# Attention scores of two batches: three float16 products on 64 rows per head in place of stacked operands on 128 rows

## The chip, the cores and the metric

One Trainium2 chip, one of its cores. The time is the device time of that core in microseconds, as a median of runs without a profile; spans, rows and waits come from one further, profiled execution. The core has TensorE for matrix products (PE in the rows, PEld for its weight loads), VectorE (DVE), ScalarE (ACT), GpSimd (POOL) and SyncE (SP), which here issues every DMA.

## The reference, cut to what matters

Rotary attention over 4 batches of 8 heads, 576 positions and 64 numbers per head, and a gated two-layer network on its output:

```python
q_rot, k_rot = (rotate(q), rotate(k))
scores = scale * np.matmul(q_rot, k_rot.transpose(0, 1, 3, 2))
scores = scores - np.max(scores, axis=-1, keepdims=True)
attn = np.exp(scores)
attn = attn / (np.sum(attn, axis=-1, keepdims=True) + 1e-09)
out = np.matmul(attn, v)
...
x = np.ascontiguousarray(out.transpose(0, 2, 1, 3)).reshape(B * S, H * D)
gate = 1.0 / (1.0 + np.exp(-(x @ w_gate)))
val = x @ w_val
return (gate * val @ w_out).astype(np.float32)
```

## The kernel before, in words

Everything is computed on one core. Heads are taken in pairs (`NP` = 4 pairs per batch), one head on partitions 0 to 63 and the other on 64 to 127. For a pair, `keys_queries` loads keys and queries, turns them by the rotary angles and, in batches 2 and 3, splits each into a float16 high part and a float16 rest (`scaled` on ScalarE, `rest` on VectorE). `score_mm` computes the scores of a tile of 128 positions of both heads against all 576 positions, in two column halves of 288; four such tiles and one of 64 positions (t = 4, both heads in one PSUM tile) make a pair. `softmax` reads the scores from PSUM (VectorE, line 505: minimum and copy), takes the exponential (ScalarE, 510), and splits the result into float16 parts; DMA transposes turn it (537), and `weigh` multiplies by the values (matmuls of line 547, target `pv`). `hidden` (matmuls of line 598, target `m`) and `project` (line 632) are the network.

Scores of batches 0 and 1 are float32 products: per column half one matmul for each head, on the 64 rows where the head lies, each of them two MATMUL instructions in a trace (line 470). Scores of batches 2 and 3 are products of float16 parts, high by high, high by rest and rest by high. So that one matmul on all 128 rows does two of these three, eight DMAs per pair (lines 449 to 455) copy the parts from the buffer `sw`, where the split left them, to `stk`, which holds for each head a stack of two parts of the queries and two stacks of the keys; each head then needs two matmuls per column half (line 482), one task for each head. The float32 operands of batches 0 and 1 lie in the same memory as `stk`.

The order of the work is not written by hand. Each piece is a task with an engine, a supposed cost in microseconds and a rank; `Plan` plays these tasks through once, when the kernel is built, and each engine then gets its instructions in the order in which they started there. A changed cost or a merged task can thus move instructions on every engine. On the chip each engine works through its own list in order and waits where data aren't there.

The scores go to two PSUM tiles, `s_ps[0]` and `s_ps[1]`, one for each head of the pair; there is no second pair of them. Three PSUM tiles `m` serve the network.

Of the kernel before, what the change touches and what calls it, by code (L numbers as in the profile page):

```python
# [156 lines left out]
def rope_attention_then_sigmoid_glu(ctx: ExitStack, tc: tile.TileContext, qk, v, w_in, w_out, tables, out):  # L157
# [17 lines left out]
    row = sb("row", [128, 32])  # L175
    pt = [sb(f"pt{i}", [128, 18, (256, 320)[i]], F16) for i in range(2)]

    stk = sb("stk", [128, 3, 2, 3, S], F16)

    flat = stk.rearrange("p n h m c -> p (n h m c)").bitcast(F32)  # L180
    qk0 = [flat[:, 2 * S * n:2 * S * n + 2 * S].rearrange("p (m c) -> p m c", m=2) for n in range(NP)]
    qkr = [sb(f"qk{n}", [128, 2, S]) for n in range(2)]
    sw = [sb(f"sw{n}", [128, 2, S]) for n in range(2)]
    p32 = [sb(f"p32{n}", [128, S]) for n in range(3)]
# [214 lines left out]
    def keys_queries(b, p, rank):  # L399

        z = ring("sw", 2)
        Z = [("sw", z, m) for m in range(2)]
        if b < NW:
            x, X = qk0[p], [("stk", n) for n in range(8 * p, 8 * p + 8)]
            X = [X[0:4], X[4:8]]
        else:
            r = ring("qk", 2)
            x, X = qkr[r], [[("qk", r, m)] for m in range(2)]
        y = sw[z]
        early = -8.5 if b == p == 0 else rank - 0.1  # L410
        dma(early, [], X[0] + X[1], 576, lambda: Y.dma_start(out=x, in_=qk[b, p, 0]))
        dma(early, [], Z, 576, lambda: Y.dma_start(out=y, in_=qk[b, p, 1]))
        gate = ["tab"] + ([("ws", 8 + p)] if b == 1 else [])
        places = [("POOL", c_pool(S, two=True))] if b > 1 else [("DVE", c_dve(S, two=True))]
        for m in range(2):
            either(places, rank, gate, X[m], lambda E, m=m: E.tensor_tensor(  # L416
                out=x[:, m], in0=x[:, m], in1=tab[:, 0], op=ALU.mult))
            either(places, rank, gate, [Z[m]], lambda E, m=m: E.tensor_tensor(  # L418
                out=y[:, m], in0=y[:, m], in1=tab[:, 1], op=ALU.mult))
            either(places, rank, [Z[m]], X[m], lambda E, m=m: E.tensor_tensor(  # L420
                out=x[:, m], in0=x[:, m], in1=y[:, m], op=ALU.add))
        if b < NW:
            slots[b, p] = p, None, -1.0 / D ** 0.5
            return
        X = X[0] + X[1]
        t, k = ring("stk", 3), ring("q_m", 4)
        M = ("q_m", k)
        e16 = y.rearrange("p m c -> p (m c)").bitcast(F16).rearrange("p (n c) -> p n c", n=4)
# [11 lines left out]
        for m, hi, lo in ((0, 1, 2), (1, 0, 3)):  # L440
            op("ACT", c_act(S), rank, [X[m], Q], Z, lambda E, m=m, hi=hi: scaled(A, e16[:, hi], x[:, m], q_s[:, k, m:m + 1]))
            op2(c_dve(S, two=True), rank, [X[m], Q], Z, lambda E, m=m, hi=hi, lo=lo: rest(
                e16[:, lo], x[:, m], q_s[:, k, m:m + 1], e16[:, hi]))
        W = [("stk", n) for n in range(12 * t, 12 * t + 12)]
        for h in range(2):
            U = W[6 * h:6 * h + 6]
            hs = slice(64 * h, 64 * h + 64)
            dst = stk[:, t, h]
            dma(rank, Z, U[0:2], 216, lambda hs=hs, dst=dst: Y.dma_start(
                out=dst[0:64], in_=e16[hs, 0:3]), U)  # L450
            dma(rank, Z, U[2:3], 72, lambda hs=hs, dst=dst: Y.dma_start(
                out=dst[64:128, 0], in_=e16[hs, 3]), U)
            dma(rank, Z, U[3:4], 72, lambda hs=hs, dst=dst: Y.dma_start(
                out=dst[64:128, 1], in_=e16[hs, 2]), U)
            dma(rank, Z, U[4:6], 72, lambda hs=hs, dst=dst: Y.dma_start(
                out=dst[64:128, 2], in_=e16[hs, 1]), U)
        slots[b, p] = t, se, se


    def score_mm(b, p, t, heads, rank):  # L460

        n = slots[b, p][0]
        if b < NW:
            kT, qT = qk0[n][:, 0], qk0[n][:, 1]

            def both(rows, width, to):
                for c in range(2):
                    for e in range(2):
                        hs = slice(64 * e, 64 * e + 64)
                        T.matmul(s_ps[to[e]][hs if width == 64 else slice(0, 128), c, 0:288], lhsT=qT[hs, rows:rows + width],  # L470
                                 rhs=kT[hs, c * 288:c * 288 + 288], start=True, stop=True)
            R = [("stk", m) for m in range(8 * n, 8 * n + 8)]
            to = heads if t < 4 else heads * 2
            mm(0.84 * len(heads), rank, R, [("s", h) for h in heads],
               lambda: both(t * 128, 128 if t < 4 else 64, to))
            return

        def one(e, o, rows, width):
            q, k, ks = (stk[:, n, e, m] for m in range(3))
            for c in range(2):  # L480
                for m, kk in enumerate((k, ks)):
                    T.matmul(o[:, c, 0:288], lhsT=q[:, rows:rows + width], rhs=kk[:, c * 288:c * 288 + 288],  # L482
                             start=(m == 0), stop=(m == 1))
        R = [[("stk", m) for m in range(12 * n + 6 * e, 12 * n + 6 * e + 6)] for e in range(2)]
        if t < 4:
            for e in range(2):
                mm(4 * c_pe(288), rank, R[e], [("s", heads[e])], lambda e=e: one(e, s_ps[heads[e]], t * 128, 128))
        else:
            h = heads[0]
            mm(8 * c_pe(288), rank, R[0] + R[1], [("s", h)], lambda: [  # L490
                one(e, s_ps[h][64 * e:64 * e + 64], 512, 64) for e in range(2)])

    def softmax(b, p, t, u, rank):

# [270 lines left out]
```

## Time and profile before

| | |
|---|---|
| median of three runs | 735.48 us (735.28 to 738.73) |
| span of the profiled execution, first to last instruction | 733.1 us |
| what lies around the span, if that execution ran as the median | 2.4 us |
| TensorE matmul busy | 632.3 us, 86% of the span |
| VectorE busy | 526.3 us, 72% |
| ScalarE busy | 462.8 us, 63% |
| GpSimd busy | 74.8 us, 10% |
| DMA moved | 100.55 MB, 54.4% of 16 engines' span in the main queue |

Busy shares are averages over stages that differ: the first quarter of the span, in which the weights are decoded and batch 0 goes through attention, leaves TensorE idle for long stretches; in most of the rest TensorE has no gap. A row's mean duration of a matmul contains the way through the array, so matmuls that follow each other overlap; the time that one costs in a stream is read from start to start.

### The profile page before, as it was taken

How to read it: one execution, taken by the hardware profiler on the slowest of the kernel's cores; microseconds unless marked ns; L12 is line 12 of the kernel's file. 1: busy time of each engine (PE TensorE's matmuls, PEld its weight loads, DVE VectorE, ACT ScalarE, POOL GpSimd, SP SyncE). 2: the span in 40 equal slices, each digit the busy share in tenths (PEclk: the TensorE clock that was granted, in tenths of full speed). 3: DMA queues.
4: the chain of work that ended last, by engine and by line, in shares of the span. 5: the costliest groups of instructions: out<-in, count | busy, mean ns of one | idle time of the engine just before them, and what ended most of it. 6: DMA issues, size and time to landing. Idle time of an engine off the chain costs nothing.

```text
span 733.1 us, 12435 instructions
## 1 busy us (share of the span) xinstructions
PE 632.3 (86%) x4642; PEld 414.7 (57%) x4642; DVE 526.3 (72%) x1194; ACT 462.8 (63%) x940; POOL 74.8 (10%) x54
## 2 busy tenths in 40 slices
PE   2355885873279999999999999999999999999997
PEld 1133573551146754577657765578667756866753
DVE  6998899988988973688879998688948574421320
ACT  3767899886556984577758768676757564322320
POOL 0400000000031100014313130131300000000000
PEclk9976697786589999999999999999999999999999
DMA  9965744746934174389596779966483534000001
GB/s 365 318 140 148 233 130 165 198 128 175 255 106 130 34 176 113 86 175 190 130 199 140 160 147 195 202 149 138 105 187 90 118 70 115 1 2 29 1 9 35
DMA packets 187484, 100.55 MB, mean 137 GB/s; under 512 B 171040, under 2 KB 176288, under 8 KB 185376
## 3 DMA queue, kind: packets, MB, share of 16 engines
q1 hardware_dynamic: 187424, 99.77, 54.4%
q8 instruction: 36, 0.59, 0.3%
q14 instruction: 24, 0.20, 0.1%
HBM read 43.12 MB, written 4.72 MB: 65 GB/s over the span
## 4 chain that ended last, share of the span: by engine, by line
PE 73%; DVE 18%; DMA 4%; issue 2%; ACT 2%; SPq 0%; DVEq 0%; ACTq 0%
PE m L598 34%; PE m L632 19%; PE pv L547 9%; PE s L470 5%; PE s L482 5%; DVE p L281 3%; DMA pt<-p 3%; DVE p L505 2%; DVE wo L298 2%; DVE wo L302 2%; DVE sw L418 1%; DVE stk L420 1%; DVE w L281 1%; DMA sw<-in_qk_dram 1%; DVE wo L295 1%
## 5 line engine op out<-in xcount | busy, mean ns | idle before, releaser
L598 PE MATMUL m<-xt,w 128*128 128x320 f16 (+1 forms) x2304 | 303.6, 290 | 8.0 <-ACT w L275 2.6
L598 PEld LDWEIGHTS <-w 128*128 128x128 f16 x2304 | 224.9, 99 | 79.2 <-issue 14.9
L632 PE MATMUL m<-wo,gt 128*128 128x512 f16 x648 | 145.9, 380 | 0.0
L510 ACT ACTIVATE p<-p,st 128x576 f32<-128x576 f32 x144 | 110.6, 769 | 51.8 <-DVE p L505 43.4
L281 DVE SCALAR_TENSOR_TENSOR p<-p,st,p 128x576 f16<-128x576 f32 x144 | 117.2, 845 | 21.9 <-ACT p L275 21.3
L470 PE MATMUL s<-stk 64*128 64x288 f32 (+1 forms) x320 | 70.0, 508 | 52.7 <-DVE p L505 38.2
L275 ACT ACTIVATE p<-p,st 128x576 f16<-128x576 f32 x144 | 104.3, 764 | 14.6 <-DVE st L515 3.5
L632 PEld LDWEIGHTS <-gt 128*128 128x128 f16 x648 | 62.1, 98 | 73.1 <-issue 4.0
L547 PE MATMUL pv<-pt,v 128*64 128x256 f16 (+3 forms) x960 | 77.1, 312 | 21.5 <-DMA pt<-p 21.5
L608 DVE SCALAR_TENSOR_TENSOR th<-th,m 128x256 f32<-128x256 f32 (+1 forms) x96 | 43.1, 450 | 67.7 <-PE m L598 66.1
L275 ACT ACTIVATE gt<-th,c_s 128x256 f16<-128x256 f32 (+1 forms) x96 | 50.3, 528 | 50.0 <-DVE th L608 49.5
L547 PEld LDWEIGHTS <-v 128*64 128x64 f16 (+1 forms) x960 | 54.1, 118 | 44.7 <-issue 29.1
L470 PEld LDWEIGHTS s<-stk 64*128 64x128 f32 (+1 forms) x320 | 35.4, 210 | 76.6 <-DVE p L505 47.5
L604 ACT ACTIVATE th<-m,gsc 128x256 f32<-128x256 f32 (+1 forms) x96 | 47.1, 493 | 36.6 <-PE m L598 35.4
L281 DVE SCALAR_TENSOR_TENSOR gt<-th,c_s,gt 128x256 f16<-128x256 f32 (+1 forms) x96 | 53.4, 562 | 19.1 <-ACT gt L275 19.0
L505 DVE TENSOR_SCALAR_CACHE_REDUCE p<-s,q_e 128x576 f32<-128x576 f32 x72 | 57.5, 812 | 10.6 <-PE s L482 10.0
L505 DVE TENSOR_SCALAR_CACHE_REDUCE p<-s 128x576 f32<-128x576 f32 x72 | 53.4, 751 | 15.0 <-PE s L470 14.5
L418 POOL TENSOR_TENSOR sw<-sw,tab 128x576 f32<-128x576 f32 x16 | 25.4, 1590 | 264.7 <-DVE xm L556 174.1
L482 PE MATMUL s<-stk 128*128 128x288 f16 (+1 forms) x320 | 44.4, 288 | 0.4 <-DVE p L505 0.4
L416 POOL TENSOR_TENSOR qk<-qk,tab 128x576 f32<-128x576 f32 x16 | 25.1, 1593 | 181.0 <-DMA qk<-in_qk_dram 137.5
L275 ACT ACTIVATE o<-m,o_s 128x512 f32<-128x512 f32 x16 | 11.0, 685 | 42.2 <-PE m L632 42.0
L482 PEld LDWEIGHTS <-stk 128*128 128x128 f16 (+1 forms) x320 | 27.4, 100 | 13.9 <-issue 5.4
(94 smaller groups left out, 508.8 us busy)
## 6 DMA issues: line engine op xcount, KB each, us to landing
wo<-in_w_dram SPq DMA_DIRECT2D x12, 1024.0 KB, 5.6
sw<-in_qk_dram SPq DMA_DIRECT2D x16, 576.0 KB, 5.1
xt<-in_wo_dram SPq DMA_DIRECT2D x12, 512.0 KB, 4.4
stk<-in_qk_dram SPq DMA_DIRECT2D x8, 576.0 KB, 4.5
xt<-in_v_dram SPq DMA_DIRECT2D x4, 1152.0 KB, 6.6
qk<-in_qk_dram SPq DMA_DIRECT2D x8, 576.0 KB, 6.0
out_dram<-o SPq DMA_DIRECT2D x16, 256.0 KB, 2.2
stk<-sw SPq DMA_DIRECT2D x16, 216.0 KB, 3.6
```

The lines of the kernel that those rows point to most:

```text
L275: A.activation(o, src, AF.Copy, scale=scale)
L281: V.scalar_tensor_tensor(out=o, in0=src, scalar=scale, in1=hi, op0=ALU.mult, op1=ALU.subtract)
L418: either(places, rank, gate, [Z[m]], lambda E, m=m: E.tensor_tensor(out=y[:, m], in0=y[:, m], in1=tab[:, 1], op=ALU.mult))
L470: T.matmul(s_ps[to[e]][hs if width == 64 else slice(0, 128), c, 0:288], lhsT=qT[hs, rows:rows + width], rhs=kT[hs, c * 288:c * 288 + 288], ...
L482: T.matmul(o[:, c, 0:288], lhsT=q[:, rows:rows + width], rhs=kk[:, c * 288:c * 288 + 288], start=(m == 0), stop=(m == 1))
L505: lambda E, h=h, c=c: V.tensor_scalar(out=p32[prs[c]].rearrange("p (c n) -> p c n", c=2), in0=s_ps[h][:, :, 0:288], scalar1=down, scalar2= ...
L510: lambda E, c=c: A.activation(p32[prs[c]], p32[prs[c]], AF.Exp, bias=st[:, k, 0, c:c + 1], scale=-1.0, accum_out=st[:, k, 1, c:c + 1]))
L547: T.matmul(v_ps[64 * e:64 * e + 64, 0:n], lhsT=v16[hs, p, a, g, :], rhs=pt[z][hs, c * 9 + g, 0:n], start=(first and m == 0), stop=(last an ...
L598: T.matmul(m_ps[m][:, 0:n], lhsT=w16[:, f, g, a, cc, :], rhs=x[:, cc, c, c0:c0 + n], start=(k == 0), stop=(k == 11))
L604: op("ACT", c_act(n), rank - 0.05, [("m", m), ("gsc", b, f)], [("th", r)], lambda E, m=m: A.activation(t, m_ps[m][:, 0:n], AF.Tanh, scale= ...
L608: op("DVE", c_dve(n, psum=True), rank - 0.05, [("m", m)], [("th", r)], lambda E, m=m: V.scalar_tensor_tensor(out=t, in0=t, scalar=1.0, in1 ...
L632: T.matmul(m_ps[m], lhsT=gt[:, f, a, c0:c0 + 128], rhs=wo16[:, f, c, :], start=(f == 0 and k == 0), stop=(f == NF - 1 and k == 2))
```

## The change

`stk` and the stacking DMAs go. `big`, four buffers of keys and queries, holds the float32 operands of batches 0 and 1 and, for batches 2 and 3, seen as float16 (`half`), high part and rest of each; the split writes there directly. A score tile of batches 2 and 3 is now one task for both heads: for each of the three terms and each column half one matmul per head, on that head's 64 rows. The supposed costs of the score tasks in `Plan` change too, for batches 0 and 1 as well (1.68 or 0.84 before, 1.2 now), and the buffers that order one task behind another are now the four `big` instead of the three `stk`.

```diff
-    stk = sb("stk", [128, 3, 2, 3, S], F16)
...
+    big = [sb(f"big{n}", [128, 2, S]) for n in range(NP)]
+    half = [t.rearrange("p m c -> p (m c)").bitcast(F16).rearrange("p (m a c) -> p m a c", m=2, a=2) for t in big]
...
-        t, k = ring("stk", 3), ring("q_m", 4)
+        t, k = ring("big", NP), ring("q_m", 4)
...
-        W = [("stk", n) for n in range(12 * t, 12 * t + 12)]
-        for h in range(2):
-            U = W[6 * h:6 * h + 6]
-            hs = slice(64 * h, 64 * h + 64)
-            dst = stk[:, t, h]
-            dma(rank, Z, U[0:2], 216, lambda hs=hs, dst=dst: Y.dma_start(
-                out=dst[0:64], in_=e16[hs, 0:3]), U)
...
+        for m in range(2):
+            h, R = half[t][:, m], [("big", t, m)]
+            op("ACT", c_act(S), rank, [X[m], Q], R, lambda E, m=m, h=h: scaled(A, h[:, 0], x[:, m], q_s[:, k, m:m + 1]))
+            op2(c_dve(S, two=True), rank, [X[m], Q], R, lambda E, m=m, h=h: rest(
+                h[:, 1], x[:, m], q_s[:, k, m:m + 1], h[:, 0]))
...
-            q, k, ks = (stk[:, n, e, m] for m in range(3))
-            for c in range(2):
-                for m, kk in enumerate((k, ks)):
-                    T.matmul(o[:, c, 0:288], lhsT=q[:, rows:rows + width], rhs=kk[:, c * 288:c * 288 + 288],
-                             start=(m == 0), stop=(m == 1))
...
+            todo = [(half[n][:, 0, a], half[n][:, 1, c]) for c, a in TERMS]
+
+        def both():
+            for m, (kT, qT) in enumerate(todo):
                 for c in range(2):
                     for e in range(2):
                         hs = slice(64 * e, 64 * e + 64)
                         T.matmul(s_ps[to[e]][hs if width == 64 else slice(0, 128), c, 0:288], lhsT=qT[hs, rows:rows + width],
-                                 rhs=kT[hs, c * 288:c * 288 + 288], start=True, stop=True)
...
+                                 rhs=kT[hs, c * 288:c * 288 + 288], start=(m == 0), stop=(m == len(todo) - 1),
+                                 skip_group_check=True)
+        mm((0.6 if b < NW else 0.42) * 2, rank, [("big", n, m) for m in range(2)], [("s", h) for h in heads], both)
```

What stands in TensorE's list for the first score tile of batch 2, before the change: the four products of one head (`s_112` is the first head's PSUM tile), with a weight load ahead of each.

```order
3095 L482 LDWEIGHTS stk
3096 L482 MATMUL s_112<-stk 128x288
3097 L482 LDWEIGHTS stk
3098 L482 MATMUL s_112<-stk 128x288
3099 L482 LDWEIGHTS stk
3100 L482 MATMUL s_112<-stk 128x288
3101 L482 LDWEIGHTS stk
3102 L482 MATMUL s_112<-stk 128x288
```

The four of the other head (`s_113`) follow at 3122, behind a small matmul and nine of line 632.

The same tile after the change (line 459 is now the matmul of all scores, `s_115` and `s_116` are the two heads' PSUM tiles, `big_73` is the first `big`):

```order
3078 L459 LDWEIGHTS big_73
3079 L459 MATMUL s_115<-big_73 128x288
3080 L459 LDWEIGHTS big_73
3081 L459 MATMUL s_116<-big_73 128x288
3082 L459 LDWEIGHTS big_73
3083 L459 MATMUL s_115<-big_73 128x288
3084 L459 LDWEIGHTS big_73
3085 L459 MATMUL s_116<-big_73 128x288
```

Sixteen more rows of the same pattern follow, up to 3101: twelve matmuls of both heads in turn, with nothing between them.

On SP's list, in batch 1's attention, the stacking stood between the transposes (537) and the loads of the next pair (411, 412), before the change:

```order
96 L534 DMA p_81<-p_81 64x2x576
97 L412 DMA sw_76<-in_qk_dram 128x1152
98 L449 DMA stk<-sw_77 64x1728 x2
99 L411 DMA qk_75<-in_qk_dram 128x1152
100 L537 DMA_TRANSPOSE pt_72<-p_81 128x18x64
101 L451 DMA stk<-sw_77 64x576 x2
102 L537 DMA_TRANSPOSE pt_72<-p_82 128x18x128
103 L453 DMA stk<-sw_77 64x576 x2
104 L537 DMA_TRANSPOSE pt_72<-p_81 128x18x128
105 L455 DMA stk<-sw_77 64x576 x2
```

After it (the transpose is line 508, the loads are 408 and 409, the copy of the 64-position tile is 505), the list of the same stretch has the loads and the transposes alone:

```order
89 L408 DMA qk_78<-in_qk_dram 128x1152
90 L505 DMA p_84<-p_84 64x2x576
91 L508 DMA_TRANSPOSE pt_72<-p_84 128x18x64
92 L508 DMA_TRANSPOSE pt_72<-p_85 128x18x128
93 L409 DMA sw_80<-in_qk_dram 128x1152
94 L508 DMA_TRANSPOSE pt_72<-p_84 128x18x128
```

VectorE's list also moves. Just ahead of the reduction that ends batch 0's attention (556, last of its eight), before the change:

```order
318 L302 SCALAR_TENSOR_TENSOR wo_62<-wo_62,xt_65 128x512
319 L420 TENSOR_TENSOR stk<-stk,sw_76 128x576
320 L505 TENSOR_SCALAR p_78,st<-s_112 128x576
321 L505 TENSOR_SCALAR p_79,st<-s_113 128x576
322 L416 TENSOR_TENSOR stk<-stk,tab 128x576
323 L281 SCALAR_TENSOR_TENSOR xt_64<-pv,xt_64 128x320
324 L556 TENSOR_REDUCE xm<-xt_64 128x1
```

After it (476 reads the scores, 293 to 300 decode an output weight, 279 is the split, 527 the reduction):

```order
318 L417 TENSOR_TENSOR big_75<-big_75,sw_79 128x576
319 L476 TENSOR_SCALAR p_81,st<-s_115 128x576
320 L476 TENSOR_SCALAR p_82,st<-s_116 128x576
321 L293 TENSOR_SCALAR wo_62<-xt_65 128x512
322 L296 SCALAR_TENSOR_TENSOR wo_62<-wo_62,xt_65 128x512
323 L300 SCALAR_TENSOR_TENSOR wo_62<-wo_62,xt_65 128x512
324 L484 TENSOR_SCALAR st<-st 128x2
325 L279 SCALAR_TENSOR_TENSOR xt_64<-pv,xt_64 128x320
326 L527 TENSOR_REDUCE xm<-xt_64 128x1
```

Over all that stands ahead of that reduction, three decoding instructions and one small one have come in and one multiplication by the rotary table (416) has gone behind it.

## Rows read from the trace of the kernel before

**Rows 1.** Busy time by stretch: engine, us busy, instructions; PEclk is the granted clock.

```profile
core 0 of [0], span 733.1 us
core 0: us, PE busy (x) PEld busy (x) DVE busy (x) ACT busy (x) POOL busy (x), PEclk, DMA share, GB/s
0.00:209.00 209.00, 118.24 (x736) 77.34 (x736) 183.86 (x376) 151.23 (x304) 7.90 (x10) 0.79 0.70 207
209.00:255.00 46.00, 42.72 (x302) 28.69 (x299) 41.40 (x88) 34.52 (x72) 12.92 (x8) 1.00 0.26 65
255.00:606.00 351.00, 348.95 (x2755) 228.62 (x2754) 269.38 (x657) 243.50 (x504) 53.99 (x36) 1.00 0.66 145
606.00:733.00 127.00, 122.42 (x857) 80.09 (x855) 31.67 (x75) 33.52 (x62) 0.00 (x0) 1.00 0.10 27
```

**Rows 2.** TensorE's matmuls by form from 255 to 606 us: busy, mean ns.

```profile
L482 PE MATMUL s<-stk 128*128 128x288 f16 x256 | 39.0, 287 | 0.4 <-DVE p L505 0.4
L470 PE MATMUL s<-stk 64*128 64x288 f32 x96 | 14.9, 429 | 0.0
L482 PE MATMUL s<-stk 128*64 128x288 f16 x64 | 5.5, 292 | 0.0
L470 PE MATMUL s<-stk 64*64 64x288 f32 x32 | 4.8, 415 | 0.0
```

**Rows 3.** Waits of TensorE's matmuls from 255 to 606 us: total, times, longest.

```profile
PE m L598 <- DVE xt L281: 0.7, 1, 0.7
PE m L598 <- ACT th L604: 0.6, 1, 0.6
PE s L482 <- DVE p L505: 0.4, 1, 0.4
PE m L598 <- ACT xt L275: 0.2, 1, 0.2
```

**Rows 4.** The stacking DMAs on SP's queue: durations ns min/median/max, first and last start.

```profile
L449 SPq DMA_DIRECT2D stk<-sw x16: 461/553/1058, 315.7 to 566.6; - x16
...
L455 SPq DMA_DIRECT2D stk<-sw x16: 583/592/602, 326.7 to 580.2; - x16
```

**Rows 5.** VectorE's groups from 255 to 606 us, and three from 100 to 209.

```profile
L505 DVE TENSOR_SCALAR_CACHE_REDUCE p<-s,q_e 128x576 f32<-128x576 f32 x71 | 56.7, 812 | 10.6 <-PE s L482 10.0
L281 DVE SCALAR_TENSOR_TENSOR sw<-qk,q_s,sw 128x576 f16<-128x576 f32 x16 | 12.9, 809 | 0.6 <-ACT sw L275 0.6
...
L298 DVE SCALAR_TENSOR_TENSOR wo<-wo,xt 128x512 int32<-128x512 int32 x10 | 6.9, 692 | 0.7
...
L416 DVE TENSOR_TENSOR stk<-stk,tab 128x576 f32<-128x576 f32 x7 | 5.3, 752 | 0.0
L295 DVE TENSOR_SCALAR wo<-xt 128x512 int32<-128x512 int32 x10 | 4.2, 418 | 0.0
```

**Rows 6.** TensorE's timeline, three stretches: start, us to the last one's end, count.

```profile
395.07 1.14 PE L482 MATMUL s<-stk 128*128 128x288 f16 x8
396.05 1.79 PE L598 MATMUL m<-xt,w 128*128 128x320 f16 x12
397.68 0.66 PE L482 MATMUL s<-stk 128*128 128x288 f16 x4
...
400.51 1.79 PE L598 MATMUL m<-xt,w 128*128 128x320 f16 x12 [0.55 <-ACT th L604]
402.23 2.35 PE L547 MATMUL pv<-pt,v 128*64 128x320 f16 x30
...
416.76 0.69 PE L482 MATMUL s<-stk 128*64 128x288 f16 x8
417.39 0.45 PE L598 MATMUL m<-xt,w 128*128 128x320 f16 x2
```

**Rows 7.** The same for single pairs of a float32 score tile, in narrow windows.

```profile
343.03 0.51 PE L470 MATMUL s<-stk 64*128 64x288 f32 x2
...
343.37 0.41 PE L470 MATMUL s<-stk 64*128 64x288 f32 x2
...
343.62 0.41 PE L470 MATMUL s<-stk 64*128 64x288 f32 x2
```

**Rows 8.** Weight loads by form from 255 to 606 us: busy, mean ns.

```profile
L482 PEld LDWEIGHTS <-stk 128*128 128x128 f16 x256 | 24.2, 98 | 11.5 <-issue 3.0
L470 PEld LDWEIGHTS s<-stk 64*128 64x128 f32 x96 | 8.3, 186 | 4.2 <-issue 1.9 <-DVE st L513 0.5 <-DVE gt L281 0.4
```

**Rows 9.** The first pair of a 64-position tile, and the first two, in narrow windows.

```profile
416.76 0.33 PE L482 MATMUL s<-stk 128*64 128x288 f16 x2
...
416.76 0.45 PE L482 MATMUL s<-stk 128*64 128x288 f16 x4
```

**Rows 10.** The chain that ended last, near the end of batch 0's attention.

```profile
195.06 4.89 DMA p<-p
...
199.97 3.92 DMA pt<-p
...
203.93 4.26 PE pv L547 x28
```

**Rows 11.** SP's transposes from 185 to 206 us: durations ns min/median/max.

```profile
L537 SPq DMA_TRANSPOSE pt<-p x3: 1723/2020/5512, 185.6 to 200.0; - x3
```

More of the change, by code (lines that the diff above doesn't have):

```diff
@@ L176, in rope_attention_then_sigmoid_glu @@
     pt = [sb(f"pt{i}", [128, 18, (256, 320)[i]], F16) for i in range(2)]
-    stk = sb("stk", [128, 3, 2, 3, S], F16)
-    flat = stk.rearrange("p n h m c -> p (n h m c)").bitcast(F32)
-    qk0 = [flat[:, 2 * S * n:2 * S * n + 2 * S].rearrange("p (m c) -> p m c", m=2) for n in range(NP)]
+    big = [sb(f"big{n}", [128, 2, S]) for n in range(NP)]
+    half = [t.rearrange("p m c -> p (m c)").bitcast(F16).rearrange("p (m a c) -> p m a c", m=2, a=2) for t in big]
     qkr = [sb(f"qk{n}", [128, 2, S]) for n in range(2)]
@@ L403, in keys_queries @@
         if b < NW:
-            x, X = qk0[p], [("stk", n) for n in range(8 * p, 8 * p + 8)]
-            X = [X[0:4], X[4:8]]
+            x, X = big[p], [[("big", p, m)] for m in range(2)]
         else:
@@ L425, in keys_queries @@
         X = X[0] + X[1]
-        t, k = ring("stk", 3), ring("q_m", 4)
+        t, k = ring("big", NP), ring("q_m", 4)
         M = ("q_m", k)
-        e16 = y.rearrange("p m c -> p (m c)").bitcast(F16).rearrange("p (n c) -> p n c", n=4)
         for m in range(2):
@@ L439, in keys_queries @@
             out=se, in0=q_i[:, k, 0:1], scalar=-1.0 / D ** 0.5, in1=q_i[:, k, 1:2], op0=ALU.mult, op1=ALU.mult))
[L440 to L443, printed above, removed]
-        W = [("stk", n) for n in range(12 * t, 12 * t + 12)]
-        for h in range(2):
-            U = W[6 * h:6 * h + 6]
-            hs = slice(64 * h, 64 * h + 64)
-            dst = stk[:, t, h]
-            dma(rank, Z, U[0:2], 216, lambda hs=hs, dst=dst: Y.dma_start(
-                out=dst[0:64], in_=e16[hs, 0:3]), U)
[L451 to L456, printed above, removed]
+        for m in range(2):
[3 more added lines that the diff above has]
+                h[:, 1], x[:, m], q_s[:, k, m:m + 1], h[:, 0]))
         slots[b, p] = t, se, se
@@ L462, in score_mm @@
         n = slots[b, p][0]
+        rows, width = t * 128, 128 if t < 4 else 64
+        to = heads if t < 4 else heads * 2
         if b < NW:
-            kT, qT = qk0[n][:, 0], qk0[n][:, 1]
-            def both(rows, width, to):
+            todo = [(big[n][:, 0], big[n][:, 1])]
+        else:
+            todo = [(half[n][:, 0, a], half[n][:, 1, c]) for c, a in TERMS]
+        def both():
+            for m, (kT, qT) in enumerate(todo):
                 for c in range(2):
@@ L470, in both @@
                         T.matmul(s_ps[to[e]][hs if width == 64 else slice(0, 128), c, 0:288], lhsT=qT[hs, rows:rows + width],
-                                 rhs=kT[hs, c * 288:c * 288 + 288], start=True, stop=True)
[L472 to L478, printed above, removed]
-            q, k, ks = (stk[:, n, e, m] for m in range(3))
-            for c in range(2):
-                for m, kk in enumerate((k, ks)):
-                    T.matmul(o[:, c, 0:288], lhsT=q[:, rows:rows + width], rhs=kk[:, c * 288:c * 288 + 288],
-                             start=(m == 0), stop=(m == 1))
[L484 to L491, printed above, removed]
+                                 rhs=kT[hs, c * 288:c * 288 + 288], start=(m == 0), stop=(m == len(todo) - 1),
+                                 skip_group_check=True)
+        mm((0.6 if b < NW else 0.42) * 2, rank, [("big", n, m) for m in range(2)], [("s", h) for h in heads], both)
     def softmax(b, p, t, u, rank):
```

## The prediction

> **What bounds the kernel now.** I read the stretches first, because a share over the whole span mixes stages [rows 1]. Up to 209 us TensorE is busy 118 of 209 us at a mean granted clock of 0.79 of 2.4 GHz (a mean over stretches at 1.2 and at 2.4), and VectorE 184: here VectorE's list and the chain through the DMAs decide. From 209 us on the clock stands at 1.00, 2.4 GHz, and from 255 to 606 us TensorE is busy 348.95 of 351 us. The float16 scores, 320 matmuls, lie wholly in that last stretch [rows 2]. There TensorE's list is the bound: its waits [rows 3] come to 1.9 us in all, one of them, 0.4 us, ahead of a float16 score. From 606 us to the end no score is left, and TensorE runs the network alone. So the change is worth what it does to TensorE's own work between 255 and 606 us, plus what its new order does to the stage before 209 us.
>
> **What it takes away without a gain.** The 64 stacking DMAs cost SP some 0.55 to 0.59 us of issue each, some 37 us in all, between 315.7 and 581 us [rows 4]. In those 350 us no matmul waits for a DMA [rows 3], so shorter ways to the scores, earlier transposes and a freer DMA system are worth nothing: the cover is TensorE's own full list. Were TensorE to run dry there, they would be worth something; nothing shows that it does. The eight splits per engine and batch stay as they are: the rest costs VectorE 809 ns [rows 5] into `sw` and the same form goes into `big`; I take 0.
>
> **The matmuls.** One 128-position tile of both heads was eight matmuls on 128 rows: 395.07 to 396.05 us, 0.98 us or 0.1225 us each [rows 6]. Now it is twelve on 64 rows, the two heads in turn. What two heads on 64 rows each do is seen in the float32 scores, the nearest row: two MATMULs stand as one entry of 0.51 us, as long as one of them, and the next pair follows from 343.37 to 343.62 us, 0.25 us later [rows 7]: the two run side by side. That float16 pairs in a tiled array go at the speed of one is seen in the 64-position tile, two heads on 64 columns each: eight matmuls in 0.63 us [rows 6], 0.49 for four pairs at 0.1225 and 0.14 that I come to below. So I take 0.1225 us for a pair: six pairs, 0.735 us, 0.245 less than before, over 32 tiles (4 tiles, 4 pairs, 2 batches) **-7.8 us**. The other end, no overlap at all, is twelve times 0.1225.
>
> The 64-position tiles lose. They already ran as four pairs side by side (64 matmuls in [rows 2], 8 for each of 8 tiles); three terms make six pairs of them: 0.245 us more, times 8, **+2.0 us**.
>
> **The changes of the array's shape.** Twelve matmuls of line 598 that are followed by others on 128 rows and 128 columns take 1.63 us (396.05 to 397.68); the same twelve ahead of line 547, which works on 64 columns, take 1.72 (400.51 to 402.23) [rows 6]: 0.09 us for a change of shape. Behind the 64-position tile it shows again: it is most of the 0.14 us above. The stacked tiles of 128 positions had the network's own shape and paid nothing of it. I counted the neighbours with different shapes in TensorE's two lists: 205 before, 256 now, and 51 more times 0.09 is **+4.6 us**. The Trainium skill (TensorEngine Tiling (Array Packing), "Key Properties") says that changing the tiling mode drains the engine, and the trace agrees, with 0.09 us. Its table "Theoretical Speedup" promises up to twofold for 64 rows; by that alone the scores would give back the 5.8 us net and nothing would be paid.
>
> Behind such a change the first weights are not loaded ahead. In the float32 tile the first pair takes 0.34 us (343.03 to 343.37) where the next takes 0.25 [rows 7], 0.09 more with loads of 186 ns [rows 8]; in the float16 tile on 64 columns the second pair ends 0.12 us behind the first, and the first lasts 0.33 us [rows 9] where one matmul of this form lasts 0.29 [rows 2], so 0.02 to 0.04 more. Float16 loads of 128 columns take 98 ns on 128 rows [rows 8]; nearer to the second, I take 0.04 us for 32 tiles, **+1.3 us**, with 0.02 and 0.09 (0.6 and 2.9) as ends.
>
> **The combined task.** Before, one head's scores needed one free PSUM tile; now a tile's products start when VectorE has read both, at 812 ns each [rows 5]. What is held up behind the waiting matmul is the network, for whose `m` ScalarE and VectorE wait in turn. The float32 tiles of batch 1 had exactly this combined form, 16 of them between 255 and 606 us (128 MATMULs, eight each, [rows 2]), and not one waited for line 505 [rows 3]. I take **+0.5 us**, with 0 below; above, one read late at every fourth of 40 tiles, 8 us.
>
> **The stage before 209 us.** The new costs reorder it. Ahead of the reduction that ends batch 0's attention VectorE now has one decoding more (418 + 692 + 692 ns, line 302 taken as its neighbour 298) and one small instruction of at most 0.2 us, less one multiplication of 752 ns [rows 5]: some 1.2 us more. In the chain, though, that time belongs to the copy `p<-p` and the transpose behind it, 4.89 and 3.92 us [rows 10], not to VectorE; so I take 0. The bounds come from SP there: one of three transposes held its queue for 5.51 us against a median of 2.02 [rows 11]. If the new order avoids that, 3.5 us are won, and if it meets it once more, lost.
>
> **Sum.** -7.8 + 2.0 + 4.6 + 1.3 + 0.5 + 0 = +0.6 us, on a span of 733.1, so 733.7, and with 2.4 us around it 736.1. The profiled span and the median of the runs (735.48, up to 738.73) agree if those 2.4 us are start and end; I add to the median: **736.1 us**.
>
> **The rivals.**
> *The drains are not all paid.* Their cost is read next to matmuls of 256 to 512 columns; where a score follows the values' product, a change was paid already. If hardly any were paid, the gain is 7.8 - 2.0 = 5.8 us: 729.7. Against it: the 0.09 us is there at both kinds of border I looked at. Chance 6%.
> *The early order wins*: the 3.5 us of SP's held queue and up to 1 us of VectorE's own, 731 to 732. For it, that stage has 91 us in which TensorE is idle; against it, VectorE's list ahead of its end is longer, not shorter. Chance 10%. The same mishap the other way, 739 to 741: 8%.
> *The pairs do not run at full speed* (slower than before). With float16 each pair brings results twice as often as the float32 pair, to both heads' PSUM tiles, and loads twice as often. If the two loads of 98 ns go one after the other, a pair takes 0.196 us in place of 0.1225, and 240 pairs cost 17.6 us: 754; halfway, 745; with no overlap of the products, 29.4 us, 766. It decides from 0.14 us a pair on (240 times 0.0175 is 4.2 us). Against it: float32 loads of 186 ns in both row halves fit into 0.25 us, so they overlap. Chance 9%.
> *The combined tasks wait* (slower than before). Ten tiles with one read of 0.81 us to wait for: 8 us, 744. It decides from five such waits on. The places are those where only twelve matmuls of the network, 1.6 us, lie between two score tiles. Against it batch 1. Chance 9%.
> That nothing happens because the transfers were hidden anyway is part of the forecast.
>
> **How the numbers follow.** The forecast, within some 3 us of 736.1, has 58%. About 0.5%, 3.7 us, is what a measurement of this kernel can tell from no change. Faster by more: 6 + 10 = 16%. Slower by more: 8 + 9 + 9 = 26%. Same: 58%. For 8 in 10 I reach down into the early order's gain and the half-paid drains, 730.5, and up over the waiting tasks, 744; outside remain the full drains saved and the pairs without overlap.
>
> **What would show it.** Right: pairs of line 459 in float16 with starts 0.12 to 0.13 us apart; tiles of 128 positions that take 0.83 to 0.95 us to the next group, those of 64 some 0.87; twelve matmuls of the network ahead of a score in 1.72 instead of 1.63 us; TensorE still busy over 99% from about 255 to 606 us, with under 3 us of waits; the DMA share there down from 0.66; the last reduction of batch 0 within 3 us of its place near 209 us. Wrong: pairs wider apart than 0.14 us; waits of line 459 for line 476 beyond 3 us; the full stretch of TensorE beginning some microseconds earlier or later; or TensorE no longer full after 300 us, in which case the transfers' removal could count after all.

## The result, and the profile after

The changed kernel takes 743.69 us (median of four runs, 742.34 to 746.51), the kernel before, on the same chip, 735.38 us (733.84 to 738.73): a ratio of 1.0128, 95% interval 1.0084 to 1.0172 (the quotient of the two medians alone is 1.0113). It is slower by some 8 us; 736.1, no change, was forecast. The profiled execution took 744.39 us, with a span of 742.6, so it is near the median.

The first three stretches of [rows 1] again, with its columns, now of the changed kernel:

```profile
0.00:209.00 209.00, 114.51 (x698) 73.61 (x699) 182.82 (x373) 150.83 (x303) 7.90 (x10) 0.83 0.71 203
209.00:255.00 46.00, 43.05 (x303) 28.98 (x303) 39.31 (x79) 30.36 (x63) 18.87 (x12) 0.96 0.31 98
255.00:606.00 351.00, 344.35 (x2911) 218.74 (x2910) 275.94 (x665) 245.38 (x509) 49.98 (x32) 1.00 0.54 124
```

From 255 to 606 us TensorE lost 4.6 us of its 348.95, although the DMA share fell from 0.66 to 0.54. The waits of TensorE's matmuls behind the last reduction of batch 0 (total, times, longest), which [rows 3] showed for most of that stretch:

```profile
PE m L569 <- ACT th L575: 2.9, 4, 1.4
PE m L569 <- DVE th L579: 2.8, 3, 1.6
PE s L459 <- DVE p L476: 2.4, 2, 1.9
PE m L569 <- DVE q_i L237: 1.0, 1, 1.0
```

They add up to 9.1 us. In the kernel before the same view, from 209 us to the end, has three lines more than the four of [rows 3], and adds up to 5.1:

```profile
PE pv L257 <- DVE row L254: 2.7, 1, 2.7
PE s L470 <- DVE p L505: 0.3, 1, 0.3
PE m L264 <- DVE wo_m L360: 0.2, 1, 0.2
```

Only 2.4 us of the 9.1 are scores that wait for a read; most are the network's own (line 569), which waits for VectorE and ScalarE. And 5.7 of the 9.1 lie before 343 us in TensorE's timeline, where batch 1 is at work; the first float16 score tile starts at 364.64 us. SP's queue near the end of batch 0's attention:

```profile
186.99 4.46 SPq L508 DMA_TRANSPOSE pt<-p  x1
...
192.68 5.89 SPq L508 DMA_TRANSPOSE pt<-p  x1
...
199.29 0.62 SPq L505 DMA_DIRECT2D p<-p  x1
...
204.41 1.98 SPq L508 DMA_TRANSPOSE pt<-p  x1
```

Two of the three transposes held the queue for over 4 us; before it was one [rows 11]. The copy `p<-p` starts at 199.29 us where it was 195.06 [rows 10], and the reduction stands at 214.24 us in VectorE's timeline, 209.09 before.

These views split the span into three: the time up to the reduction, TensorE's waits behind it, and what is left over, the rest: TensorE's work with the few microseconds at the end.

| profiled execution | last reduction | waits | rest | span |
|---|---|---|---|---|
| before | 209.1 | 5.1 | 518.9 | 733.1 |
| after | 214.2 | 9.1 | 519.3 | 742.6 |
| difference | +5.1 | +4.0 | +0.4 | +9.5 |

TensorE's work, on which nearly all of the forecast was spent, is as forecast. The time was lost in the two places that had been given 0 and 0.5 us.

The cut between the two is not a clean one, and it makes the early loss look larger than it is. TensorE first needs what follows from the reduction at the matmul `pv<-row`, which spreads batch 0's largest value. In the kernel before, VectorE decodes an output weight between the reduction and that matmul, beside GpSimd, which sets in at 209.69 us with four instructions, and TensorE waits 2.72 us; in the changed kernel this decoding stands ahead of the reduction, and nothing waits. Before, and behind the dots after:

```profile
210.19 1.72 DVE L298 SCALAR_TENSOR_TENSOR wo<-wo,xt 128x512 int32<-128x512 int32 x1
211.95 1.78 DVE L302 SCALAR_TENSOR_TENSOR wo<-wo,xt 128x512 f32<-128x512 f32 x1
213.65 1.95 DVE L418 TENSOR_TENSOR sw<-sw,tab 128x576 f32<-128x576 f32 x1
215.84 0.38 PE L257 MATMUL pv<-row,ones 1*128 1x1 f32 x2 [2.72 <-DVE row L254]
...
218.20 0.38 PE L255 MATMUL pv<-row,ones 1*128 1x1 f32 x2
```

At this matmul the changed kernel is 2.4 us late, not 5.1; behind it TensorE waits 6.7 us more (9.1 against 2.4), and the rest is 0.4 longer.

**The products themselves.** A tile's first two, four and six matmuls, from three narrow windows (start, us to the last one's end):

```profile
474.54 0.30 PE L459 MATMUL s<-big 64*128 64x288 f16 x2
474.54 0.42 PE L459 MATMUL s<-big 64*128 64x288 f16 x4
474.54 0.54 PE L459 MATMUL s<-big 64*128 64x288 f16 x6
```

One pair more, 0.12 us more: the two heads run side by side at the speed of one. (The stacks of the kernel before held rest by rest too: their eight matmuls of a tile did four products, not only three; the twelve of the change do three.) TensorE's timeline for whole tiles:

```profile
385.40 0.91 PE L459 MATMUL s<-big 64*128 64x288 f16 x12
386.25 1.80 PE L569 MATMUL m<-xt,w 128*128 128x320 f16 x12
...
388.29 0.92 PE L459 MATMUL s<-big 64*64 64x288 f16 x12
389.14 1.80 PE L569 MATMUL m<-xt,w 128*128 128x320 f16 x12
...
401.36 1.80 PE L569 MATMUL m<-xt,w 128*128 128x320 f16 x12
403.10 0.91 PE L459 MATMUL s<-big 64*128 64x288 f16 x12
```

From start to start a tile of 128 positions takes 0.85 us, one of 64 also 0.85, and the network's twelve ahead of a score 1.74 instead of 1.63 [rows 6].

### The profile page after: what moved, and what is told of

It is laid out like the page before. It is cut to its first block, busy times and chain, and to the rows that moved or that the text cites. A ratio compares the mean times of both kernels' runs of the same rounds, so it can differ in the third digit from the quotient of the medians.

```text
span 742.6 us, 12611 instructions
## 1 busy us (share of the span) xinstructions
PE 633.8 (85%) x4802; PEld 405.8 (55%) x4802; DVE 531.4 (72%) x1194; ACT 462.1 (62%) x940; POOL 76.8 (10%) x54
## 4 chain that ended last, share of the span: by engine, by line
PE 71%; DVE 18%; DMA 5%; ACT 4%; issue 3%; SPq 0%; DVEq 0%; ACTq 0%
PE m L569 33%; PE m L603 19%; PE s L459 9%; PE pv L518 8%; DVE p L279 3%; DMA pt<-p 3%; DVE p L476 2%; DVE wo L300 1%; DVE wo L296 1%; DVE sw L415 1%; DVE v L279 1%; DVE w L279 1%; DVE big L417 1%; DVE gt L279 1%; DMA sw<-in_qk_dram 1%
## 5 line engine op out<-in xcount | busy, mean ns | idle before, releaser
L459 PE MATMUL s<-big 64*128 64x288 f16 (+3 forms) x800 | 108.8, 379 | 55.3 <-DVE p L476 39.8
L279 DVE SCALAR_TENSOR_TENSOR p<-p,st,p 128x576 f16<-128x576 f32 x144 | 124.1, 892 | 11.9 <-ACT p L273 11.3
L459 PEld LDWEIGHTS s<-big 64*128 64x128 f32 (+1 forms) x320 | 36.1, 213 | 79.4 <-DVE p L476 49.2
L279 DVE SCALAR_TENSOR_TENSOR gt<-th,c_s,gt 128x256 f16<-128x256 f32 (+1 forms) x96 | 50.9, 537 | 18.9 <-ACT gt L273 18.8
L279 DVE SCALAR_TENSOR_TENSOR xt<-pv,xt 128x256 f16<-128x256 f32 (+1 forms) x32 | 14.5, 454 | 23.7 <-ACT xt L273 23.6
L273 ACT ACTIVATE xt<-pv 128x256 f16<-128x256 f32 (+1 forms) x32 | 13.1, 408 | 28.3 <-PE pv L518 27.9
```

What stands on the lines that cost most here:

```text
L273: A.activation(o, src, AF.Copy, scale=scale)
L279: V.scalar_tensor_tensor(out=o, in0=src, scalar=scale, in1=hi, op0=ALU.mult, op1=ALU.subtract)
```

## The experiments

The theory: the loss is in the order of the engines' lists, which the new tasks and costs changed in both stages. Its rivals: the task for both heads waits; the new products do not overlap or cost more than their rows show; the DMAs hold the transposes in any order. The letters in the expectations belong to each expectation alone. Not all runs were of one chip, so a time is compared with the kernel before in the same rounds, by its ratio.

**One term.** After, but only the product of the two high parts; the other two are left out.

```diff
-            for m, (kT, qT) in enumerate(todo):
+            for m, (kT, qT) in enumerate(todo[:1]):
```

> The changed kernel with the same lists, but the float16 scores of batches 2 and 3 keep only the product of the high parts; the two products with the rests are left out. That takes four pairs of 0.1225 us from each of 40 tiles, 19.6 us of TensorE's work. If TensorE's list is the bound behind 215 us: 723 to 728. If VectorE or ScalarE would bound it right behind: 732 or more, and TensorE's idle time grows by what is missing.

Measured: 726.28 us, ratio 0.9868 (0.9816 to 0.992), 17.4 us below the changed kernel's median, inside the 723 to 728 expected. TensorE's list is the bound, as the prediction had it. The row also gives the price of a tile:

```profile
472.98 0.42 PE L459 MATMUL s<-big 64*128 64x288 f16 x4
473.33 1.48 PE L569 MATMUL m<-xt,w 128*128 128x256 f16 x12
```

Two pairs take 0.35 us from start to start, six 0.85: 0.125 a pair and 0.10 that does not depend on their number.

**Head after head.** After, a tile's twelve float16 matmuls as six of one head and then six of the other.

```diff
+            if b >= NW:
+                turns.sort(key=lambda x: x[2])
```

> The changed kernel, with the twelve products of a float16 score tile in the order six of one head, then six of the other; nothing else moves. If two heads run side by side only when their matmuls alternate in the list: a tile of 128 positions takes about 1.5 us instead of 0.84 to the next group, 40 tiles cost some 27 us, time about 770. If TensorE takes the second head's matmuls ahead of the first's, as the 64-position tile of the kernel before looked (head after head in the list, pairs in the trace): 0.84 us and 743 to 745.

Measured: 755.06 us, ratio 1.0254 (1.0211 to 1.0297).

```profile
474.87 1.17 PE L461 MATMUL s<-big 64*128 64x288 f16 x12
475.97 2.12 PE L605 MATMUL m<-wo,gt 128*128 128x512 f16 x9
```

1.10 us a tile: between the 0.85 of full overlap and the 1.6 of none (12 times 0.125 and 0.10). Neither of the two expected times came; the truth lies between. The turn by turn of the change is needed, and it does its work: the rival that the products do not overlap is out.

**Both heads in one task, in the kernel before.** Its eight stacked matmuls of a tile as one task.

```diff
-            for e in range(2):
-                mm(4 * c_pe(288), rank, R[e], [("s", heads[e])], lambda e=e: one(...))
+            mm(8 * c_pe(288), rank, R[0] + R[1], [("s", h) for h in heads], lambda: [one(...) for e in range(2)])
```

> The kernel before, with one change: the two heads' stacked products of a 128-position tile of batches 2 and 3 are one task of eight matmuls that needs both PSUM tiles. Products, stacks and DMAs as before; the lists up to the last reduction of batch 0 are the same. Theory D (the task for both heads makes TensorE wait for VectorE's reads): TensorE idle 8 us or more behind 209 us instead of 5.3, time 738 to 740. Rival L (the waits come from where an order happens to put things, not from the joint task): idle 4 to 7 us, 735 to 737.

Measured: 735.48 us, ratio 0.9993 (0.997 to 1.0015); reduction at 209.7, waits of 4.1 us in all, 1.2 of them float16 scores. The joint task alone costs nothing here.

**The early order, from both sides.** After with the old supposed costs of batches 0 and 1, and before with the new ones. Each has the other kernel's lists up to batch 0's last reduction. Batch 1's supposed costs change with them, so the lists behind it are not kept in either.

```diff
-        mm((0.6 if b < NW else 0.42) * 2, rank, ...
+        mm(0.84 * len(heads) if b < NW else 0.84, rank, ...
```

> The changed kernel, with the supposed costs of the score tasks of batches 0 and 1 as they were before (1.68 and 0.84 instead of 1.2). All lists up to the last reduction of batch 0 are then those of the kernel before; the products and the lists behind stay those of the change. Theory A (some 5 of the 9 us are lost in the reordered stage before 215 us, 4 behind it): that reduction back at 209 us, time 738 to 740. Rival B (the products or the combined tasks of batches 2 and 3 cost it all): 743 to 745. If the early order alone is the cause: 735.

```diff
-            mm(0.84 * len(heads), rank, R, [("s", h) for h in heads],
+            mm(1.2, rank, R, [("s", h) for h in heads],
```

> The kernel before, with nothing changed but the supposed cost of the score tasks of batches 0 and 1 (1.2 for each). Its lists up to the last reduction of batch 0 are those of the changed kernel; stacks and stacking DMAs stay. Theory A: that reduction at 214 us instead of 209, time 739 to 741. Rival B: 735 to 736.

Measured: 742.29 us, ratio 1.0089 (1.0063 to 1.0116), with the reduction at 211.6 and waits of 11.1 us; and 738.29 us, 1.0033 (1.0008 to 1.0058), reduction at 212.8, waits of 4.9. The new costs cost the kernel before some 2.5 us; the old ones give the changed kernel back 1.4, within what the intervals leave open. Both are less than was expected (739 to 741, and 738 to 740). And little of it is the early order: with the new costs in the kernel before, the matmul `pv<-row` starts at 216.72 us, 0.9 later than in the kernel before, and the waits behind it are 4.9 us in place of 2.4. The larger part of the loss stays with the changed kernel whatever stands in the early lists.

**The true price of a tile in the plan.** The changed kernel with the old costs of batches 0 and 1, and 0.95 in place of 0.84 for a float16 tile.

> The changed kernel with the old supposed costs for batches 0 and 1, and for batches 2 and 3 the measured cost of a score tile with its changes of shape, 0.95 us instead of 0.84. If TensorE's later waits come from a plan in which it is too fast: idle behind the last reduction of batch 0 5 to 6 us instead of 9 to 11, time 737 to 739. If each new order simply draws its own waits: idle anywhere from 5 to 12 us, 738 to 745.

Measured: 742.71 us, ratio 1.0103 (1.0054 to 1.0151), reduction at 208.5, waits of 10.8 us. No gain.

**Loads behind the transposes.** After; on SP seven loads (the expectation says six) near the end of batch 0's attention put behind the next transpose or copy.

```diff
+        for loads, turn in [([57, 58], 59), ([60, 61], 62), ([63], 64), ([65, 66], 67)]:
```

> The changed kernel, with six loads on SP's list (output weights, and keys and queries of batch 1) put behind the transpose or copy that stood next behind them, in the last 30 us of batch 0's attention; every other list is the same. Theory A in its detail (the transposes there wait behind the loads, in SP's queue and in full DMA engines): last reduction of batch 0 at 208 to 211 us instead of 214, time 738 to 741. Rival C (the transposes wait for VectorE's splits, and the loads ahead of them cost nothing): 214 us and 743 to 744.

Measured: 743.86 us, ratio 1.0096 (1.0065 to 1.0127), reduction at 214.2. The first transpose fell to 2.09 us, the second stayed at 5.33, and VectorE got the output weights that it decodes later, so that its part of the last tile came at 199.0 us instead of 195.4; it had waited 3.2 us for one of the moved loads. With only one transpose held, as in the kernel before, and the last values' product 3.4 us earlier (205.95 instead of 209.30), the reduction did not move. A miss, and no support for the held transpose as the cause of the early loss.

**The last tile first.** After; one piece each of ScalarE's, VectorE's and SP's work for the last 64-position tile moved ahead.

```diff
+        for e, part, at in [('ACT', [218], 215), ('SP', [64], 62), ('DVE', [317], 313)]:
```

> The changed kernel with three places of the lists moved, near the end of batch 0's attention: ScalarE's high part of the last 64-position tile ahead of two decoding instructions in which it stood waiting for output weights (it ran at 193.72 us, 189.59 in the kernel before), VectorE's rest of that tile ahead of three, and the copy of that tile on SP ahead of a transpose that held the queue for 5.89 us. If the lists' order there is where the 5.1 us of the stage before 209 us were lost, the copy starts at some 194 to 196 us instead of 199.3, the last reduction of batch 0 comes near 209 to 211 us instead of 214.2, and the time is some 4 us lower, 739.5 to 740. Rival: the DMA engines are full there, in whatever order; then the copy and the transposes take as much longer as they start earlier, the reduction stays near 214, and the time at 743 to 744.

Measured: 745.07 us, ratio 1.0114 (1.0072 to 1.0155). The copy starts at 194.72 us as wanted, but a load ahead of the last transpose on SP now waits for VectorE until 201.3, the transpose's data take 6.56 us, and the reduction stands at 213.3. Moving one piece moved the wait: as an account of the early loss by that one tile, the theory of the order failed here.

**The values' product first**, and **the late places.** After; on TensorE the values' product ahead of a 64-position score near 85 and 479 us; then a set of moves near 330, 479 and 511 us.

```diff
+        for front, place in [([26, 27, 28], 25), ([290, 291, 292], 289)]:
```

> The changed kernel, with two places of TensorE's list exchanged and nothing else: the values' product that stands behind a 64-position score tile (at 85 us in batch 0, at 479 us in batch 2) is put ahead of it. At 479 us TensorE waited 1.85 us for VectorE to read the second head; at 85 us the score pushed the values' product back from 85.5 to 89 us. If those two waits are a price of the order: last reduction of batch 0 1 to 3 us earlier, no wait at 479 us, time 739 to 742. If the time comes back behind them: 743 to 744.

```diff
+        for e, part, at in [('DVE', [513], 510), ('DVE', [512], 511), ('PE', [290, 291, 292], 289), ('DVE', [826, ..., 831], 835)]:
```

> The changed kernel with four places moved behind batch 0: near 330 us the network's scale and the read of a second head ahead of a split on VectorE; near 479 us the values' product ahead of the 64-position score on TensorE; near 511 us three splits of the values, and four small instructions behind them, after the network's own that TensorE waited for. If the 4 us more of TensorE's waits are these single places of the new order, the waits behind 214 us fall from 9.3 to some 5 to 6 us and the time by 3 to 4, to 740 to 741. Rival: VectorE is short of time there throughout (three softmax buffers, splits slowed beside GpSimd), and the waits come back a few instructions later; then they stay above 8 us and the time at 743 or more.

Measured: 742.07 us, ratio 1.0094 (1.0067 to 1.0121), reduction at 213.5, waits of 6.4 us; and 743.61 us, 1.011 (1.0077 to 1.0143), waits of 8.2. By their intervals neither is told apart from the changed kernel. The second set shortened the waits it was meant for, and another came:

```profile
509.17 0.30 PE L535 MATMUL pv<-pt,v 128*64 128x256 f16 x2
512.42 0.83 PE L535 MATMUL pv<-pt,v 128*64 128x256 f16 x6 [2.95 <-DVE v L296]
```

The three splits of the values that I put behind the network's work were needed at once by the values' product. VectorE is late there, as the rival said; of the two, what was put last waited.

**Early and late moves together.** The moves of the last tile, those of the late places, and the values' product ahead of the score near 85 us.

```diff
+        for e, part, at in [('PE', [26, 27, 28], 25), ('ACT', [218], 215), ('SP', [64], 62), ('DVE', [317], 313), ...]:
```

> Both sets of moves together, and the values' product ahead of the 64-position score near 85 us. If the loss is all in the lists' order, the sum: last reduction near 209 to 211 us, waits of 5 to 6 us, TensorE's work as before, so 735 to 737, the kernel before within its uncertainty, and not faster. Rival (waits and DMA come back elsewhere): 741 to 744.

Measured: 746.08 us, ratio 1.0132 (1.0095 to 1.0169): reduction 213.2, waits 10.3, and a rest of 523.2 instead of 519.3; 735 to 737 was expected. The stretch around the wait of 2.96 us near 513 us says why the rest grew:

```profile
513.00:517.00 4.00, 1.05 (x10) 0.90 (x12) 3.74 (x5) 1.65 (x4) 3.92 (x3) 0.78 0.00 0
517.00:521.00 4.00, 4.00 (x31) 2.54 (x26) 2.58 (x6) 0.00 (x0) 0.16 (x1) 0.50 0.02 5
521.00:525.00 4.00, 4.00 (x35) 3.18 (x35) 1.05 (x4) 2.99 (x8) 0.00 (x0) 0.86 0.64 146
```

Behind the wait TensorE ran with a granted clock of 0.50, 1.2 GHz, for some five microseconds. This is what moves the rest from run to run: in the eight executions, both kernels among them, in which the clock stays at 1.00 behind 217 us, the rest is 518.4 to 519.5 us; in the seven in which it falls behind a wait, 519.9 to 523.7 (the two changes of the products, in the first experiments, left aside).

**The copy first, in the kernel before.** Only the copy of the last 64-position tile, on SP, ahead of the transpose of 5.51 us.

```diff
+        for e, part, at in [('SP', [63], 61)]:
```

> The kernel before with only one move: on SP the copy of batch 0's last 64-position tile ahead of the transpose of 5.51 us that it stood behind. If a held queue there costs the stage its time, the copy starts at 191.7 instead of 195.1 us, the last reduction comes up to 2 us earlier, and the time is 733 to 735; by the rival (the DMA engines are full in any order) 735 to 736.

Measured: 734.07 us, ratio 0.9978 (0.9956 to 1.0001), reduction at 207.0:

```profile
191.18 0.62 SPq L551 DMA_DIRECT2D p<-p  x1
191.85 1.94 SPq L554 DMA_TRANSPOSE pt<-p  x1
...
197.01 1.77 SPq L554 DMA_TRANSPOSE pt<-p  x1
```

No transpose is held. In the kernel before a held queue does cost this stage its 2 us, in the profile; in the time it is at the edge of what was resolved.

**The new products in the old order.** After, every operation as it is, with each engine's list in the order of the kernel before with one task for both heads: in place of the plan's own order a table of task and engine. Then the same with the copy first on SP, and with the changed kernel's own lists up to batch 0's last reduction and the old order from there on.

```diff
-        self.starts = self.order()
+        for k, x in enumerate(ORDER.split()):
+            lists.setdefault(ENGINES[x[-1]], []).append((k, int(x[:-1]), ENGINES[x[-1]]))
...
```

> The changed kernel, every operation as it is, but each engine's list put in the order of the kernel before with one score task for both heads (735.48 us); only the stacking transfers and their place are missing. If the order is all of the loss, the time is that of this order plus 0.3 us of TensorE's work: 735 to 737, last reduction near 209 to 210 us, waits behind it 4 to 5.5 us. Rival: the new products or the missing transfers cost the time by themselves; then 741 to 744 with waits of 9 us or more.

> As the run before, with the copy of batch 0's last 64-position tile ahead of the transpose on SP, which gave the kernel before 1.2 us. If the order is all, 734 to 736; by the rival 741 or more.

> The changed kernel with its own lists up to the last reduction of batch 0 and the old order from there on. If both stages' orders cost what their profiles differ by, the reduction stays near 213 to 214 us, the waits behind it fall to 4 to 6, and the time is 738 to 740. Rival (the new products wait in any order): 741 to 744.

Measured, in this order: 737.96 us, ratio 1.0037 (1.0012 to 1.0062); 734.09 us, 0.999 (0.9964 to 1.0017); 737.64 us, 1.0031 (1.0008 to 1.0054). The 741 to 744 of the rivals is out in all three. The last one's waits behind its reduction, which stands at 211.5 us:

```profile
PE s L472 <- DVE p L489: 4.1, 5, 2.2
PE m L582 <- DVE th L592: 0.4, 1, 0.4
PE m L275 <- DVE wo_m L371: 0.2, 1, 0.2
```

The network's waits have all but gone, and 4.7 us are left in all, of which 3.8 are float16 scores waiting for a read: in the old order the joint task does wait, more than in the kernel before (0.4). So the order it is, and mostly that of the lists behind batch 0's last reduction. With the new products, medians in us:

| | new late order | old late order |
|---|---|---|
| new early order | 743.69 | 737.64 |
| old early order | 742.29 | 737.96 |

The kernel before took 735.38 us beside the two on the left and 734.8 beside the two on the right, so they stand 8.3, 6.9, 2.8 and 3.2 us above it: the late order is worth 5.5 and 3.8 us, the early one 1.4 and -0.3, which is not resolved.

## Why the prediction was wrong

**What bounds the kernel: right.** Two thirds of the products less gave 17.4 us back, though TensorE was the only engine relieved. The DMA share fell to 0.54, and no gain came with it.

**The matmuls: right.** 0.12 to 0.125 us a pair, 0.85 us a 64-position tile (0.63 and 0.245 were put at 0.875). The rival of pairs not at full speed is out.

**The changes of shape and the first weights: right in their sum.** The part of a tile that does not grow with its pairs is 0.10 us (in the prediction's terms, the change of shape and the first weights together), and the network's twelve ahead of a score take 0.11 more; 0.09 and 0.04 had been taken. All terms of TensorE's work came to +0.1 us, and the rest of the span grew by 0.4. The Trainium skill (TensorEngine Tiling (Array Packing), "Key Properties") says that a change of mode drains the engine; the trace agrees, with 1.74 us for the network's twelve ahead of a score instead of 1.63.

**The combined task, +0.5 us: this is the step that failed.** It asked only whether the scores wait for a read, and let all other waits of [rows 3] stand as they were. But the new plan moved VectorE's, ScalarE's and TensorE's lists behind 209 us too, and I had priced the new order only ahead of it. What came is 4.0 us more of waits behind the reduction, 6.7 behind `pv<-row`, and most of them are the network's: 5.7 us of the 9.1 wait for `th`. The joint task by itself, in the stacked kernel, costs nothing. The rival "the combined tasks wait" gave the right time, 744, by luck: it counted ten reads of scores, and 2.4 us of scores waited. Rows of the kernel before can tell what an operation costs, not what a list will wait for that does not exist yet; that is read by laying the two orders side by side over the whole stretch in which the bound engine has no slack.

Where VectorE falls behind can be seen at one of the places, VectorE and GpSimd near 511 us of the changed kernel:

```profile
511.03 5.46 DVE L279 SCALAR_TENSOR_TENSOR v<-xt,v_s,v 128x576 f16<-128x576 f32 x3
516.41 1.37 DVE L541 TENSOR_SCALAR gsc<-w_i,v_i 128x12 f32<-128x12 f32 x1
...
510.69 1.41 POOL L413 TENSOR_TENSOR qk<-qk,tab 128x576 f32<-128x576 f32 x1 [44.11 <-ACT v L273]
512.19 1.80 POOL L417 TENSOR_TENSOR qk<-qk,sw 128x576 f32<-128x576 f32 x1
513.95 1.92 POOL L413 TENSOR_TENSOR qk<-qk,tab 128x576 f32<-128x576 f32 x1
515.95 1.79 POOL L417 TENSOR_TENSOR qk<-qk,sw 128x576 f32<-128x576 f32 x1
```

and what it cost TensorE:

```profile
514.78 2.79 PE L569 MATMUL m<-xt,w 128*128 128x256 f16 x24
519.15 1.47 PE L569 MATMUL m<-xt,w 128*128 128x256 f16 x12 [1.57 <-DVE th L579]
```

Three splits of a form that takes 0.8 us each elsewhere [rows 5] took 1.8, beside four instructions of the rotation on GpSimd, and the network's `th` stood behind them. The Trainium skill (GPSIMD Engine Reference, "1. Specifications") says that GpSimd shares its SBUF interfaces with VectorE and contends with instructions of two SBUF inputs; the trace agrees, with 1.8 against 0.8 us. The old order has such a meeting too, at 210 us, and TensorE's wait of 2.72 us hangs on it. That this contention is the cause of the late loss as a whole is argued from this place, not shown: no run took GpSimd out.

**The stage before 209 us, 0 us: missed by 5.1 us at the reduction, by 2.4 at the matmul that uses it.** The rival "the same mishap the other way, 739 to 741" fits what the profile of the changed kernel shows, one more transpose that holds SP; but with that transpose free the reduction did not move, so the cause of the early delay stays open. Its size in the time is smaller. Executions with the new early lists untouched have the reduction at 214.2, 212.0, 211.5, 211.2, 212.8 and, in the kernel before, 212.8; those with the old ones at 209.1, 209.7, 211.6, 210.2 and 208.5. The means are 2.6 us apart; at `pv<-row` they are 216.5 and 215.8, 0.7 apart. In the medians the early order counted for -0.3 and 1.4 us.

**The sum, as the runs have it.** 0.4 us of work, 0.7 for the early order, and some 5.9 for the late one (waits behind `pv<-row` of 9.1, 9.4 and 9.1 us with lists that the plan makes for the new tasks, of 2.4, 2.4, 3.9 and 4.7 with the old): 7.0 us, where the medians differ by 8.3 and the interval allows 6.2 to 12.6. What lies around the span, taken as 2.4 us, is 1.8 in the changed kernel's runs; the two profiled spans differ by 9.5.

**What stays open.** Which part of the plan's new input makes the late order worse; the joint task alone costs nothing in the stacked kernel, the old costs and a higher price of a tile do not give the loss back, and the missing transfers and the four buffers were not tried apart. No run has the old order in batch 1's stretch alone, up to some 343 us, where most of the waits lie. The new products in the old order are 2.7 us slower than the kernel before, of which the profiles show 1.1 in the reduction's place, 0.2 in the waits and 1.3 in the rest, where the granted clock fell to 0.64 from 381 to 385 us behind a wait of 2.32; with the copy first they take 0.999 of the kernel before, which with the copy first takes 0.9978. No version beat both kernels by more than its interval.

## What to carry to other kernels

Where a planner sets the order, a changed cost or a merged task is two changes: the operations, which rows of the old trace can price, and a new order of every list, which they can't. Price the first, then read the new order on every engine over the whole stretch in which the bound engine runs without slack; and run the new operations once in the old order, before the change is judged: here that turned 1.0128 into 1.0037. Single moves in the changed kernel's full lists gave back nothing that was resolved: mostly they moved the wait.

## What the runs showed of the hardware that was not expected

- Six matmuls of one head and then six of the other still overlapped in part: 1.10 us a tile, between 0.85 and 1.6.
- Behind single waits in an otherwise full stretch TensorE's granted clock fell in some executions: to 0.50 behind 2.96 us (the window above), to 0.57 behind 1.35 us (the true price in the plan, 337 to 341 us) and behind 1.85 (the last tile first, 485 to 489 us). In others it stayed at 1.00: behind 1.85 us at 479 us in the changed kernel, behind 2.25 at 379 us with the old late order.
- The same transpose held SP for 5.51 us in the kernel before and took 1.94 us with the copy ahead of it.
- A VectorE instruction on 12 columns took 1.37 us beside GpSimd in the changed kernel, and 0.35 us in the kernel before at 506.11 us, where GpSimd was at work too (505.02 to 507.81 us): not every instruction beside GpSimd is slowed.
